# The opening of a Fourier-attention and ELU kernel, laid out anew

## The chip, the cores and the metric

The kernel runs on one core of one Trainium2 chip. The core has five instruction streams that run side by side and meet only at semaphores: TensorE (PE, matrix products into PSUM), VectorE (DVE), ScalarE (ACT), GpSimd (POOL) and SyncE (SP, which here only issues DMAs; POOL and ACT issue some too). The metric is the device time of one launch in microseconds. Before the change three timed runs gave 903.19, 903.33 and 905.1 us, median 903.33.

## What is computed

Two stages. The first mixes each of 8 sequences (3008 positions, 256 channels) in the frequency domain; the second sends the 24064 rows through 256 -> 2048 -> 256 with an ELU between.

```python
X = np.fft.rfft(x, axis=1)
Yr = Xr @ w_r - Xi @ w_i + b_r
Yi = Xr @ w_i + Xi @ w_r + b_i
lam = 0.01                                   # soft threshold of both parts
Yr = np.sign(Yr) * np.maximum(np.abs(Yr) - lam, 0.0)
Yi = np.sign(Yi) * np.maximum(np.abs(Yi) - lam, 0.0)
y = np.fft.irfft(Yr + 1j * Yi, n=x.shape[1], axis=1)
...
h = x @ w_in
g = np.where(h > 0.0, h, np.exp(np.minimum(h, 0.0)) - 1.0)
return (g @ w_out).astype(np.float32)
```

## The kernel before

The transform of length 3008 = 47 x 64 is done as matrix products in two steps each way, with the twiddle factors built into the matrices M1 to M4. For one sequence the work is cut into these units:

- **A** (6 units, `unit_A`, L150): the transform over the 64, two matmuls of 512 columns into two PSUM banks, copied to a tile A. Four j-blocks per unit; two units share one tile A of 8 blocks, and its store to the DRAM tensor DA reorders the data. `load_Z` (L172) reads it back as Z.
- **X** (8 units, `unit_X`, L187): the transform over the 47, eight small matmuls, copied into XT. Two channel halves (dt) times four groups of eight.
- **M** (12 groups, `m_group`, L205 and L210): the product with the weights, 128 rows by 512 columns; then the soft threshold, which gives Y. A tile Y holds two groups. In the opening the threshold is done either as bias in PE, Relu in ACT (L245, `clip`) and a minimum in DVE (L235, done late by `let_go`), or by a DVE add (L220) and two POOL instructions (L248, L249).
- **B** (6 units, L262 or, as `split_B`, L326): the first inverse step, eight matmuls per unit into two banks, copied to a tile Bz (for the first pair of units under the tag A) and stored to DB by SP (L278, L338). `load_Bs` (L295) reads DB back as four tiles Bs.
- **Y** (8 units, L403, L416, L430): the second inverse step, into yT.

The second stage walks 376 steps, 47 for each sequence (a step is one block of 512 rows and one pair of the 16 blocks of 128 hidden columns): `front` (L895) makes the hidden values, ACT takes the exponential (L902 in the first ten steps), POOL or DVE finish the ELU (L948, L937), and `back` (L969), two steps later, adds into the output banks. The work of the next sequence, units A to Y, is dealt out over the steps by `plan`: list `f0` stands before a step's `front`, list `f1` behind it.

The instruction order of each engine is the order in which the source issues it; nothing reorders it. Every engine takes its own list in order, so an instruction that waits holds up all behind it. Tiles come from pools with a tag and a number of buffers: `wk2` has two for each tag (A and Bz among them), `wk3` three, and a tile that reuses a buffer waits for all reads of it, a DMA's landing included. PSUM has eight banks, shared out anew in stages: `pre2` and `pre1` up to the M groups, `lateB`, `chain` and `lateA` after them, then `psO`, `psS0`, `psS1` and `psG`.

The opening is all that comes before the steps of sequence 0 can run: A, X and M of sequence 0, all B units, the first quarter of Y, and the loads and scaling of w_in. The first Y quarter needs rows of all B units; those of B 0, 1 and 2 (48 of the 96 rows, `NT` = 3) are not waited for through DRAM but turned on chip: `turn_B` (L366) makes them with the channels in the partitions, `turn_back` (L385) turns them with the identity into Bs, and only the rows of B 3 to 5 come by `load_Bs(0, 0, 48)`. The order of M groups is 3, 4, 5, 0, 1, 2, with B 3, B 4 and B 5 between them. Then come turn_B(0), group (2, 1), B 0, turn_B(1), B 1 as a split unit, turn_B(2), two turn_backs, a spare A unit of sequence 1 (`spare_A`, L307), first_Y (L403), B 2 (L326), and the steps. In steps 0 to 4 the remaining five A units of sequence 1 run, in steps 7 to 9 the other quarters of Y of sequence 0, and from step 10 on X of sequence 1.

`idle_pe` (L445) are matmuls whose result is not used. `gate` (L750) is a POOL copy of one column, which keeps POOL's next DMA behind the tile that it reads; the second half of w_out (`load_w_out(1)`, L737) is loaded by POOL behind such a gate on Bs.

Of the kernel before, what the change touches and what calls it, by code (L numbers as in the profile page):

```python
# [8 lines left out]
ALU = mybir.AluOpType  # L9
# [20 lines left out]
def kernel(  # L30
# [93 lines left out]
    def evac(dst, src, on_dve):  # L124
        if on_dve:
            nc.vector.tensor_copy(dst, src)
        else:
            nc.scalar.copy(dst, src)  # L128
# [109 lines left out]
    def first_M(q, i, on_act):  # L238

        ps = pre1.tile([P, 2 * D], F32, name="mps1", tag="mps1")  # L240
        yb, clip = m_group(0, q, i, ps[:], on_act)
        let_go()
        Y_ = Y_of[0, q][:, i, :]
        if on_act:
            nc.scalar.activation(clip[:], yb, AF.Relu, bias=lam_n[:])  # L245
            held.append((Y_, yb, clip))
        else:
            nc.gpsimd.tensor_scalar(clip[:], yb, LAM, -LAM, ALU.min, ALU.max)  # L248
            nc.gpsimd.tensor_tensor(Y_, yb, clip[:], ALU.subtract)  # L249

    def unit_B(b, v, alone=False, on_dve=False):
        if (b, v // 2) not in Bz_of:
            t = "A" if alone and v == 0 else "Bz"
            Bz_of[b, v // 2] = wk2.tile([P, 8, D], BF16, name=t, tag=t)
            if b not in DB_of:
                DB_of[b] = dram.tile([K1, P, D], BF16, name="DB", tag="DB")
        Bz, Y = Bz_of[b, v // 2], Y_of.pop((b, v))
        ps = unit_ps("bps", alone)
        for pp in range(2):
            for c in range(2):  # L260
                for s in range(2):
                    nc.tensor.matmul(  # L262
                        ps[:, s, pp * D : pp * D + D],
                        lhsT=M3[s * N2 : s * N2 + N2, 2 * v + pp, c, :],
                        rhs=Y[s * N2 : s * N2 + N2, pp, c * D : c * D + D],
                        start=(c == 0), stop=(c == 1),
                    )
        o = 4 * (v % 2)
        Bv = Bz[:, o : o + 4, :].rearrange("p (q s) d -> p s q d", s=2)
        psv = ps[:].rearrange("p s (q d) -> p s q d", d=D)  # L270
        if on_dve:
            nc.scalar.copy(Bv[:, :, 0], psv[:, :, 0])
            nc.vector.tensor_copy(Bv[:, :, 1], psv[:, :, 1])
        else:
            nc.scalar.copy(Bv, psv)  # L275
        if alone:
            k0 = 4 * v
            nc.sync.dma_start(  # L278
                DB_of[b][k0 : k0 + 4].rearrange("k p d -> p k d"), Bz[:, o : o + 4, :]
            )  # L280
        elif b == 1 and v > 3:
            nc.sync.dma_start(
                DB_of[b][4 * v : 4 * v + 4].rearrange("k p d -> p k d"), Bz[:, o : o + 4, :]
            )
        elif v % 2:
            k0 = 8 * (v // 2)
            nc.sync.dma_start(DB_of[b][k0 : k0 + 8].rearrange("k p d -> p k d"), Bz[:])
# [10 lines left out]
    def two_banks(pool, n):  # L298
        return [pool.tile([P, 512], F32, name=n, tag=n) for _ in range(2)]

    def spare_A():

        A_of[1, 0] = wk2.tile([P, 8, D], BF16, name="A", tag="A")
        DA_of[1] = dram.tile([NJ, P, D], BF16, name="DA", tag="DA")
        ps = two_banks(lateA, "lateA")
        for j in range(2):
            nc.tensor.matmul(  # L307
                ps[j][:], lhsT=M1[:], rhs=xts[0][:, 2 * j : 2 * j + 2, :], start=True, stop=True
            )

        def store():
            for j in range(2):
                evac(
                    A_of[1, 0][:, 2 * j : 2 * j + 2, :].rearrange("p n d -> p (n d)"),
                    ps[j][:], bool(j),
                )

        return store

    def split_B(v, ps, both_dve):  # L320

        Bz, Y = Bz_of[0, v // 2], Y_of.pop((0, v))
        for pp in range(2):
            for c in range(2):
                for s in range(2):
                    nc.tensor.matmul(  # L326
                        ps[s][:, pp * D : pp * D + D],
                        lhsT=M3[s * N2 : s * N2 + N2, 2 * v + pp, c, :],
                        rhs=Y[s * N2 : s * N2 + N2, pp, c * D : c * D + D],
                        start=(c == 0), stop=(c == 1),  # L330
                    )
        o = 4 * (v % 2)
        Bv = Bz[:, o : o + 4, :].rearrange("p (q s) d -> p s q d", s=2)

        def store():
            for s in range(2):
                evac(Bv[:, s], ps[s][:].rearrange("p (q d) -> p q d", d=D), both_dve or bool(s))
            nc.sync.dma_start(  # L338
                DB_of[0][4 * v : 4 * v + 4].rearrange("k p d -> p k d"), Bz[:, o : o + 4, :]
            )  # L340

        return store
# [4 lines left out]
    def one_bank():  # L347
        return chain.tile([P, 512], F32, name="one", tag="one")

    def turn_B(v, ps=None):  # L350

        split = ps is not None

        if not turned:
            turned.append(wk3.tile([P, 2, 8, 16 * NT], BF16, name="yb", tag="yb"))
        Y, T = Y_of[0, v], turned[0]
        if split:
            ps = [t[:, 0:P] for t in ps]
        else:
            both = unit_ps("tps", True)  # L360
            ps = [both[:, s, 0:P] for s in range(2)]
        for pp in range(2):
            for dt in range(2):
                for c in range(2):
                    for s in range(2):
                        nc.tensor.matmul(  # L366
                            ps[s].rearrange("p (t m q g) -> p t q g m", t=2, m=8, q=2)[:, dt, pp],
                            lhsT=Y[
                                s * N2 : s * N2 + N2, pp, c * D + dt * P : c * D + dt * P + P
                            ],  # L370
                            rhs=M3[s * N2 : s * N2 + N2, 2 * v + pp, c, :].rearrange(
                                "p (g m) -> p g m", g=4
                            )[:, :, 0:8],
                            start=(c == 0), stop=(c == 1),
                        )
        Tv = T[:, :, :, 16 * v : 16 * v + 16].rearrange("p t m (q s g) -> p s (t m) q g", q=2, s=2)
        for s in range(2):
            evac(Tv[:, s], ps[s].rearrange("p (n q g) -> p n q g", q=2, g=4), split and bool(s))

    def turn_back(dt):  # L380

# [345 lines left out]
    def load_w_in(q):  # L727
        if q < 3:
            wf = late3.tile([P, 2, FQ], F32, name="w_in_f", tag="Et")
        else:  # L730
            wf = late2.tile([P, 2, FQ], F32, name="w_in_f", tag="osb")
        nc.sync.dma_start(wf[:], w_in_v[:, :, q * FQ : q * FQ + FQ])
        w_in_f.append(wf)
# [19 lines left out]
    def fB(v, on_dve=False):  # L753
        unit_B(0, v, alone=True, on_dve=on_dve)
# [9 lines left out]
    nc.scalar.copy(bias_bc[:], nb[:])  # L764
    idle_pe(5)
    for u in range(8):
        unit_X(0, u, alone=True, on_dve=u in (1, 3, 5), apart=u > 5)
        if u == 3:
            nc.vector.tensor_tensor(w3[:], v3[:], w3[:], ALU.subtract)
        if u < 6:  # L770
            idle_pe(1)
    zeroth.close()
    pre2, pre1 = (
# [30 lines left out]
    fB(4)  # L804
    scale_w_in(0, True, 0)
    first_M(0, 1, True)
    first_M(1, 0, False)
    fB(5)
    load_w_in(2)
    load_Bs(0, 0, 16 * NT)  # L810
    scale_w_in(0, True, 1)
    first_M(1, 1, True)
    first_M(2, 0, True)
    turn_B(0)
    scale_w_in(1, True, 0)
    first_M(2, 1, True)
    fB(0)
    turn_B(1)
    let_go()
    store_B = split_B(1, two_banks(pre1, "mps1"), False)  # L820
    turn_B(2, two_banks(pre1, "mps1"))
    store_B()
    load_w_in(3)
    M4v = M4[:].rearrange("p (a h) -> p a h", h=2)
    for h, w in enumerate((w40, w41)):
# [9 lines left out]
        )  # L835
        for n_, k_ in (("lateB", 2), ("chain", 4), ("lateA", 2))
    )
    turn_back(0)
    turn_back(1)
    keep_A = spare_A()  # L840
    first_Y(0)
    first_Y(1)
    keep_B = split_B(2, two_banks(lateB, "lateB"), False)
    keep_A()
    keep_B()
    scale_w_in(1, True, 1)
    second.close()

# [150 lines left out]
    def plan(b):  # L999
# [40 lines left out]
            if u == ("A", 5) and n2 < B:  # L1040
                f1[t] += [(load_Z, (n2, s0, s1)) for s0, s1 in ((0, 8), (8, NS))]
        if b == 0:
            for t in range(5):
                f1[t].append((unit_A, (1, t + 1, False, t not in (1, 2), True)))
            for t, a, u in (
                (7, f0, 2), (7, f1, 3), (8, f0, 4), (8, f1, 5), (9, f0, 6), (9, f1, 7)
            ):
                a[t].append((split_Y, (0, u)))
            for t, w in ((2, 1), (3, 2), (5, 3)):
                f1[t].append((load_Bs, (0, w)))  # L1050
            f1[5] += [(load_Z, (1, s0, s1)) for s0, s1 in ((0, 8), (8, 16), (16, NS))]
            f1[xs[0]].append((lambda: gate(Z_of[1][:, 16, 0:1]), ()))
        if n2 < B:
# [84 lines left out]
```

## Time and profile before

One execution was profiled: it took 904.25 us, its span from the first to the last instruction is 902.5 us, at a granted TensorE clock of 0.999.

| engine | busy us | share of the span | instructions |
|---|---|---|---|
| PE (matmul) | 884.6 | 98% | 6667 |
| PEld (weight load, beside PE) | 653.5 | 72% | 6770 |
| DVE | 714.4 | 79% | 902 |
| ACT | 696.8 | 77% | 871 |
| POOL | 325.0 | 36% | 464 |

The times of the opening, from the timelines (us from the start of the span):

| what | PE starts at |
|---|---|
| first X unit of sequence 0 | 24.06 |
| first M group | 30.39 |
| turn_back | 47.42 |
| first front of step 0 | 50.29 |
| first X unit of sequence 1 (step 10) | 72.66 |

How to read the lines further down. A row of the timeline is: start, duration (of all together, where several equal instructions are merged), engine, line, operation, tile written <- tiles read, shape, count, and in brackets how long the engine had been idle and what ended that. SPq, POOLq and ACTq rows are the issue of a DMA, not its transfer. A row of the waits is: who waited, for what, us in total, how many times, the longest. A row of a DMA queue is: packets, MB, share of the time of 16 DMA engines.

### The profile page before, as it was taken

How to read it: one execution, taken by the hardware profiler on the slowest of the kernel's cores; microseconds unless marked ns; L12 is line 12 of the kernel's file. 1: busy time of each engine (PE TensorE's matmuls, PEld its weight loads, DVE VectorE, ACT ScalarE, POOL GpSimd, SP SyncE). 2: the span in 40 equal slices, each digit the busy share in tenths (PEclk: the TensorE clock that was granted, in tenths of full speed). 3: DMA queues.
4: the chain of work that ended last, by engine and by line, in shares of the span. 5: the costliest groups of instructions: out<-in, count | busy, mean ns of one | idle time of the engine just before them, and what ended most of it. 6: DMA issues, size and time to landing. Idle time of an engine off the chain costs nothing.

```text
span 902.5 us, 17320 instructions
## 1 busy us (share of the span) xinstructions
PE 884.6 (98%) x6667; PEld 653.5 (72%) x6770; DVE 714.4 (79%) x902; ACT 696.8 (77%) x871; POOL 325.0 (36%) x464
## 2 busy tenths in 40 slices
PE   9899999999999999999999999999999999999997
PEld 4467667876688667876678766787667866777776
DVE  7788768877788778897788877888778877788776
ACT  6788788877878778778887887878787877776664
POOL 7561550134230531404504243133332134443664
PEclk9999999999999999999999999999999999999999
DMA  8996226621473226713266041752128111231011
GB/s 257 325 255 182 86 68 195 190 71 48 124 204 117 71 63 166 206 59 94 60 198 188 25 112 53 213 162 82 55 82 226 31 42 47 75 95 44 24 48 48
DMA packets 90489, 105.80 MB, mean 117 GB/s; under 512 B 5363, under 2 KB 81142, under 8 KB 86982
## 3 DMA queue, kind: packets, MB, share of 16 engines
q1 hardware_dynamic: 84054, 76.64, 30.4%
q0 software_dynamic: 5968, 27.26, 9.2%
q8 instruction: 53, 0.87, 0.4%
q10 hardware_dynamic: 384, 0.79, 0.3%
q14 instruction: 30, 0.25, 0.1%
HBM read 54.86 MB, written 49.81 MB: 116 GB/s over the span
## 4 chain that ended last, share of the span: by engine, by line
PE 88%; DVE 4%; ACT 3%; issue 2%; DMA 1%; POOL 0%; DVEq 0%; ACTq 0%; POOLq 0%
PE ps_o L969 35%; PE hps L895 34%; PE mps L210 9%; PE bps L262 2%; PE aps L150 2%; PE yps L430 2%; PE xps L187 2%; DVE gT L939 1%; DVE Et L950 1%; ACT Et L913 1%; ACT Et L916 1%; ACT Bz L275 1%; PE sps L895 1%; DMA Z<-DA 1%; DMA xt<-in_x_dram 0%
## 5 line engine op out<-in xcount | busy, mean ns | idle before, releaser
L969 PE MATMUL ps_o<-w_out_r,gT 128*128 128x256 f32 x3008 | 475.9, 301 | 0.1
L969 PEld LDWEIGHTS ps_o<-w_out_r,gT 128*128 128x128 f32 x3008 | 403.1, 189 | 49.0 <-DVE osb L981 1.6
L895 PE MATMUL hps<-yT,w_in_s 128*128 128x512 bf16 (+7 forms) x1613 | 372.0, 350 | 5.1 <-DVE gT L939 0.2
L937 DVE SCALAR_TENSOR_TENSOR gT<-Et,hps 128x512 fp32r<-128x512 f32 (+1 forms) x268 | 220.1, 850 | 73.8 <-POOL Et L948 37.5
L939 DVE SCALAR_TENSOR_TENSOR gT<-hps,Et 128x1024 fp32r<-128x1024 f32 x190 | 232.3, 1222 | 16.0 <-DVE Et L950 0.9
L895 PEld LDWEIGHTS <-w_in_s 128*128 128x128 bf16 x1728 | 141.5, 98 | 128.3 <-issue 21.4
L948 POOL TENSOR_SCALAR Et<-Et 128x512 f32<-128x512 f32 x204 | 121.9, 616 | 224.5 <-ACT Et L911 217.0
L916 ACT ACTIVATE Et<-hps 128x1024 f32<-128x1024 f32 x190 | 195.8, 1031 | 8.7 <-PE hps L895 2.3
L950 DVE TENSOR_SCALAR Et<-Et 128x1024 f32<-128x1024 f32 x190 | 131.4, 692 | 44.2 <-ACT Et L916 36.5
L228 POOL TENSOR_SCALAR clip<-yb 128x512 f32<-128x512 f32 x84 | 51.8, 616 | 317.3 <-DVE yb L220 279.8
L911 ACT ACTIVATE Et<-hps 128x512 f32<-128x512 f32 x182 | 98.9, 596 | 62.2 <-PE hps L895 60.5
L913 ACT ACTIVATE Et<-hps 128x1024 f32<-128x1024 f32 x84 | 86.3, 1027 | 71.8 <-PE hps L895 70.3
L229 POOL TENSOR_TENSOR Y<-yb,clip 128x512 bf16<-128x512 f32 x84 | 107.3, 1277 | 7.0
L914 ACT ACTIVATE Et<-Et 128x1024 f32<-128x1024 f32 x84 | 88.8, 1058 | 2.7
L220 DVE TENSOR_TENSOR yb<-mps,bias_bc 128x512 f32<-128x512 f32 x88 | 60.6, 689 | 36.0 <-PE mps L210 24.4
L128 ACT CAST XT<-xps 128x768 bf16<-128x768 f32 x59 | 47.2, 800 | 15.4 <-PE xps L187 15.3
L210 PE MATMUL mps<-wcat_s,XT 128*128 128x512 bf16 x182 | 56.7, 379 | 0.7
L210 PE MATMUL mps<-wcat_r,XT 128*128 128x512 bf16 x179 | 57.0, 384 | 0.4 <-ACT Bz L275 0.4
L128 ACT CAST A<-aps 128x1024 bf16<-128x1024 f32 x42 | 42.5, 1014 | 14.0 <-PE aps L150 12.5
L210 PEld LDWEIGHTS <-XT 128*128 128x128 bf16 x384 | 30.9, 98 | 30.0 <-ACT XT L128 1.2
L128 ACT CAST yT<-yps 128x752 bf16<-128x752 f32 x56 | 44.2, 789 | 9.2 <-PE yps L430 9.1
L275 ACT CAST Bz<-bps 128x1024 bf16<-128x1024 f32 x45 | 45.1, 1002 | 3.6 <-PE bps L262 3.6
(149 smaller groups left out, 463.6 us busy)
## 6 DMA issues: line engine op xcount, KB each, us to landing
xt<-in_x_dram POOLq DMA_DIRECT2D x21, 1024.0 KB, 7.1
out_dram<-osb SPq DMA_DIRECT2D x158, 128.0 KB
Bs<-DB SPq DMA_DIRECT2D x30, 384.0 KB
DA<-A SPq DMA_DIRECT2D x20, 512.0 KB
DB<-Bz SPq DMA_DIRECT2D x20, 512.0 KB
Z<-DA SPq DMA_DIRECT2D x6, 1152.0 KB
xt<-in_x_dram POOLq DMA_DIRECT2D x6, 512.0 KB, 5.7
Z<-DA SPq DMA_DIRECT2D x8, 384.0 KB
```

What stands on the lines that cost most here:

```text
L128: nc.scalar.copy(dst, src)
L210: nc.tensor.matmul(ps, lhsT=XT[:, dt, c, o : o + P], rhs=(wcat_r, wcat_s)[c][:, dt, :], start=(not biased and (c, dt) == (0, 0)), stop=((c ...
L229: nc.gpsimd.tensor_tensor(Y_of[b, q][:, i, :], yb, clip[:], ALU.subtract)
L895: nc.tensor.matmul(hps[s][:, c0:c1] if early else hps[:, s, c0:c1], lhsT=w_in_s[:, dt, ft * P : ft * P + P], rhs=yT_of[b][:, dt, t0 : t0 + ...
L911: nc.scalar.activation(E_[:, s], hps[:, s], AF.Exp)
L913: nc.scalar.activation(E_, hps[:], AF.Relu, scale=-1.0)
L916: nc.scalar.activation(E_, hps[:], AF.Exp)
L937: nc.vector.scalar_tensor_tensor(o, e, -1.0, h, ALU.add, ALU.max)
L939: nc.vector.scalar_tensor_tensor(o, h, 0.0, e, ALU.max, ALU.add)
L948: nc.gpsimd.tensor_scalar(E_[s], E_[s], 1.0, 0.0, ALU.min, ALU.max)
L950: nc.vector.tensor_scalar(E_, E_, 1.0, -1.0, ALU.min, ALU.add)
L969: nc.tensor.matmul(po[q][:, i_ % 2, :], lhsT=gT[:, s, i_ * P : i_ * P + P], rhs=w_out_r[:, ft, :], start=(ft == 0 and i_ % 2 == 0), stop=( ...
```

## The change

X: units 4 to 7 (before: 6 and 7) put their halves into two banks, of which ACT copies one and DVE the other; unit 3 goes from DVE to ACT; the subtraction for w3 comes after unit 1 and not after 3; the fillers after units 4 and 5 are gone.

M and B: B 5 and `load_Bs(0, 0, 48)` come one M group earlier, and the load of w_in's third quarter behind that Bs load in SP's queue. The last group (2, 1) becomes `last_M`: its 512 columns are done as two halves (each holds one channel half of the real and of the imaginary part) in two banks, with a clip and a minimum of its own for each. `load_w_in(3)`, the two M4 rows, the gate and `load_w_out(1)` come right after it, before the pools change. Then, from the late pools: turn_B(1), B 0, turn_B(2) in two channel halves, the store of B 0, B 1, turn_backs, B 2, first_Y, and behind them the stores of B 2 and then of B 1 (both of B 1's copies by DVE). `spare_A` is gone.

Steps: all six A units of sequence 1 lie in steps 0 to 5, and Bs 1, 2 and 3 are loaded in steps 1, 2 and 3 (before: 2, 3 and 5).

```diff
+    def last_M(q, i):
+        XT, o = XT_of[0], (2 * q + i) * P
+        clip = wk2.tile([P, 2 * D], F32, name="clip", tag="clip")
+        todo = []
+        for h, t in enumerate(two_banks(pre1, "mps1")):
+            def cols(v):
+                return v.rearrange("p (c h d) -> p c h d", c=2, h=2)[:, :, h]
+            ps = t[:, 0:D]
+            nc.tensor.matmul(ps, lhsT=busy[:, 0:P], rhs=cols(bias_p[:]), start=True, stop=False)
+            for c in range(2):
+                for dt in range(2):
+                    nc.tensor.matmul(
+                        ps, lhsT=XT[:, dt, c, o : o + P],
+                        rhs=cols((wcat_r, wcat_s)[c][:, dt, :]),
+                        start=False, stop=((c, dt) == (1, 1)),
+                    )
+            ch = clip[:, D * h : D * h + D]
+            nc.scalar.activation(ch, ps, AF.Relu, bias=lam_n[:])
...
+        let_go()
+        for Y_, yb, ch in todo:
+            nc.vector.scalar_tensor_tensor(Y_, yb, LAM, ch, ALU.add, ALU.min)
...
-    def split_B(v, ps, both_dve):
-
+    def split_B(v, ps, on_dve=(False, True)):
+
+        if (0, v // 2) not in Bz_of:
+            t = "A" if v == 0 else "Bz"
+            Bz_of[0, v // 2] = wk2.tile([P, 8, D], BF16, name=t, tag=t)
...
-                evac(Bv[:, s], ps[s][:].rearrange("p (q d) -> p q d", d=D), both_dve or bool(s))
+                evac(Bv[:, s], ps[s][:].rearrange("p (q d) -> p q d", d=D), on_dve[s])
...
-    def turn_B(v, ps=None):
+    def turn_B(v, ts=(0, 1), ps=None, on_dve=False):
...
     for u in range(8):
-        unit_X(0, u, alone=True, on_dve=u in (1, 3, 5), apart=u > 5)
-        if u == 3:
+        unit_X(0, u, alone=True, on_dve=u == 1, apart=u > 3)
+        if u == 1:
             nc.vector.tensor_tensor(w3[:], v3[:], w3[:], ALU.subtract)
-        if u < 6:
+        if u < 4:
             idle_pe(1)
...
     first_M(0, 1, True)
+    fB(5)
+    load_Bs(0, 0, 16 * NT)
+    load_w_in(2)
     first_M(1, 0, False)
-    fB(5)
-    load_w_in(2)
-    load_Bs(0, 0, 16 * NT)
...
     turn_B(0)
     scale_w_in(1, True, 0)
-    first_M(2, 1, True)
-    fB(0)
-    turn_B(1)
-    let_go()
-    store_B = split_B(1, two_banks(pre1, "mps1"), False)
-    turn_B(2, two_banks(pre1, "mps1"))
-    store_B()
+    last_M(2, 1)
     load_w_in(3)
...
+    turn_B(1, ps=two_banks(lateB, "lateB"))
+    store_0 = split_B(0, two_banks(lateA, "lateA"))
+    for t in range(2):
+        turn_B(2, (t,), two_banks(chain, "one"), True)
+    store_0()
+    store_1 = split_B(1, two_banks(lateB, "lateB"), (True, True))
     turn_back(0)
     turn_back(1)
-    keep_A = spare_A()
+    store_2 = split_B(2, two_banks(lateA, "lateA"))
     first_Y(0)
     first_Y(1)
-    keep_B = split_B(2, two_banks(lateB, "lateB"), False)
-    keep_A()
-    keep_B()
+    store_2()
+    store_1()
     scale_w_in(1, True, 1)
...
         if b == 0:
-            for t in range(5):
-                f1[t].append((unit_A, (1, t + 1, False, t not in (1, 2), True)))
+            for t in range(6):
+                f1[t].append((unit_A, (1, t, False, t not in (1, 2), True)))
...
-            for t, w in ((2, 1), (3, 2), (5, 3)):
-                f1[t].append((load_Bs, (0, w)))
+            for w in range(1, 4):
+                f1[w].append((load_Bs, (0, w)))
```

`spare_A` is taken out whole: it made the tile A and the tensor DA of sequence 1, ran the two matmuls of A unit 0 into `lateA` and left the two copies (ACT and DVE) to be done behind first_Y.

More of the change, by code (lines that the diff above doesn't have):

```diff
@@ L249, in first_M @@
             nc.gpsimd.tensor_tensor(Y_, yb, clip[:], ALU.subtract)
+    def last_M(q, i):
[16 more added lines that the diff above has]
+            nc.scalar.activation(ch, ps, AF.Relu, bias=lam_n[:])
+            todo.append(
+                tuple(
+                    v.rearrange("p (c d) -> p c d", c=2) if k else cols(v)
+                    for k, v in enumerate((Y_of[0, q][:, i, :], ps, ch))
+                )
+            )
+        let_go()
+        for Y_, yb, ch in todo:
+            nc.vector.scalar_tensor_tensor(Y_, yb, LAM, ch, ALU.add, ALU.min)
     def unit_B(b, v, alone=False, on_dve=False):
@@ L299, in two_banks @@
         return [pool.tile([P, 512], F32, name=n, tag=n) for _ in range(2)]
[L301 to L318, printed above, removed]
-    def split_B(v, ps, both_dve):
+    def split_B(v, ps, on_dve=(False, True)):
+        if (0, v // 2) not in Bz_of:
+            t = "A" if v == 0 else "Bz"
+            Bz_of[0, v // 2] = wk2.tile([P, 8, D], BF16, name=t, tag=t)
+            if 0 not in DB_of:
+                DB_of[0] = dram.tile([K1, P, D], BF16, name="DB", tag="DB")
         Bz, Y = Bz_of[0, v // 2], Y_of.pop((0, v))
@@ L348, in one_bank @@
         return chain.tile([P, 512], F32, name="one", tag="one")
-    def turn_B(v, ps=None):
-        split = ps is not None
+    def turn_B(v, ts=(0, 1), ps=None, on_dve=False):
         if not turned:
@@ L356, in turn_B @@
         Y, T = Y_of[0, v], turned[0]
+        w = len(ts) * 64
+        split = ps is not None
         if split:
-            ps = [t[:, 0:P] for t in ps]
+            ps = [t[:, 0:w] for t in ps]
         else:
             both = unit_ps("tps", True)
-            ps = [both[:, s, 0:P] for s in range(2)]
+            ps = [both[:, s, 0:w] for s in range(2)]
         for pp in range(2):
-            for dt in range(2):
+            for dt in ts:
                 for c in range(2):
@@ L366, in turn_B @@
                         nc.tensor.matmul(
-                            ps[s].rearrange("p (t m q g) -> p t q g m", t=2, m=8, q=2)[:, dt, pp],
+                            ps[s].rearrange("p (t m q g) -> p t q g m", m=8, q=2, g=4)[
+                                :, dt - ts[0], pp
+                            ],
                             lhsT=Y[
@@ L375, in turn_B @@
                         )
-        Tv = T[:, :, :, 16 * v : 16 * v + 16].rearrange("p t m (q s g) -> p s (t m) q g", q=2, s=2)
+        Tv = T[:, ts[0] : ts[-1] + 1, :, 16 * v : 16 * v + 16].rearrange(
+            "p t m (q s g) -> p s (t m) q g", q=2, s=2
+        )
         for s in range(2):
-            evac(Tv[:, s], ps[s].rearrange("p (n q g) -> p n q g", q=2, g=4), split and bool(s))
+            evac(Tv[:, s], ps[s].rearrange("p (n q g) -> p n q g", q=2, g=4), on_dve and bool(s))
     def turn_back(dt):
```

## The prediction

> **What bounds the kernel now.** First the page's part 1 and the windows: PE is busy 884.6 of 902.5 us at a granted clock of 1.00, so from the eleventh step on (72.66 us) every engine is paced by PE, and an edit of the opening can only shift that body as a whole. So the sum asks one thing: at what time does the first X unit of the next batch start, 72.66 us now? Then PE's waits between 20 and 75 us, which are all the opening has to give:
>
> ```profile
> PE mps L205 <- DVE XT L126: 1.1, 1, 1.1
> PE xps L187 <- DMA Z<-DA: 0.8, 2, 0.4
> PE one L385 <- DVE yb L126: 0.5, 1, 0.5
> PE mps L366 <- DVE Y L235: 0.3, 1, 0.3
> PE gps L150 <- ACT A L128: 0.2, 1, 0.2
> PE xps L187 <- DVE yT L126: 0.2, 1, 0.2
> ```
>
> (us in total, times, longest.) The longest is the first M group waiting for DVE's copies of X. DVE's timeline there (start, us) shows w3's subtraction and the last whole copy behind it, then two half copies that end at 30.33; PE goes on at 30.39:
>
> ```profile
> 27.59 0.95 DVE L769 TENSOR_TENSOR A<-Bz,A 128x768 f32<-128x768 f32 x1
> 28.46 0.95 DVE L126 CAST XT<-xps 128x768 bf16<-128x768 f32 x1
> 29.32 1.01 DVE L126 CAST XT<-mps 128x384 bf16<-128x384 f32 x2
> ```
>
> Next the DMA queues, since B's stores move. SP's timeline, with POOL's one row for the second half of w_out (1 MB) and ACT's copies of step 2:
>
> ```profile
> 46.68 0.36 SPq L278 DMA_DIRECT2D DB<-A  x1
> 47.94 0.36 SPq L338 DMA_DIRECT2D DB<-A  x1
> 48.34 0.50 SPq L732 DMA_DIRECT2D w_in_f<-in_moe_w_in_dram  x1
> 51.62 0.36 SPq L338 DMA_DIRECT2D DB<-Bz  x1
> 52.84 4.81 SPq L165 DMA_DIRECT2D DA<-A  x2
> 57.82 0.46 SPq L295 DMA_DIRECT2D Bs<-DB  x1
> ```
>
> ```profile
> 48.28 0.98 POOL L737 DMA_DIRECT2D w_out_r<-in_moe_w_out_dram  x1 [0.28 <-issue]
> ```
>
> ```profile
> 55.22 1.09 ACT L902 ACTIVATE Et<-sps 128x512 f32<-128x512 f32 x2 [0.44 <-PE sps L895]
> 56.19 1.08 ACT L128 CAST A<-gps 128x512 bf16<-128x512 f32 x2
> ```
>
> B 0 and 1 leave at 46.68 and 47.94, ahead of w_out; B 2 leaves at 51.62, behind it. What that means is in the DMA view of 52.6 to 54.7 us, where B 2's 512 packets had been issued and w_out's were moving:
>
> ```profile
> q0 software_dynamic: 648, 0.66, 128.5%
> q1 hardware_dynamic: 3, 0.00, 0.3%
> ```
>
> POOL's queue (q0) moved 648 packets and SP's (q1) three. And the whole stretch from 44.0 to 56.4, in which DMA had hardly a pause:
>
> ```profile
> DMA packets 3473, 3.21 MB, mean 259 GB/s; under 512 B 123, under 2 KB 2912, under 8 KB 3472
> ```
>
> **The change part by part.** *X by two engines.* (Before, DVE copies u 1, 3 and 5 whole and half of 6 and 7.) u 3 goes to ACT whole (0.80), u 4 to 7 become halves; the two 0.22 us fillers behind u 4 and 5 filled a wait and cost nothing gone. PE still meets u 4 at 27.33 (the Z wait stays). DVE then has L769 done by 27.1 and four halves, 0.46 us apart by the row of 1.01 for two, the first at 27.9: 27.9 + 3 x 0.46 + 0.55 = 29.83 in place of 30.33. ACT's halves (0.86 for two) end sooner. Gain 0.5. Bounds: 0 if u 6 and 7, which reuse the banks of u 4 and 5, wait longer for them, 1.1 if the whole wait went; 0.5, since I can count it.
>
> *M groups, B 5 one group earlier.* Same PE rows. B 5 stands at about 39.25; its Y is ready at 39.43 - 0.5 = 38.9: no wait. The load of Bs (0,0) then leaves ahead of w_in 2 in SP's queue, about 0.7 us sooner (it waits for B 5's store, which is behind B 4's), and is no longer behind w_in 2's transfer, worth as much again. First_Y has 1.5 us of room. Cost 0; without that cover 0.7 at most.
>
> *Last M group in halves, B 0 to 2 in its waits.* Ten matmuls of 256 for five of 512 is the same 1.08 us. ACT's clip (0.69) and DVE's min (0.69) become two halves of about 0.48 and 0.42 (estimates: the slope of the rows of 512 and 1024), so the first half of turn_B(2) starts 0.3 us sooner; the 0.76 us that PE idles from 45 to 48 (busy 2.24 of 3.00) is met by B 0 and B 1, which stood before it, so it is mostly moved. In order, by rows: last M ends 44.35 (44.87 - 0.5); turn 0.23, B 0 0.54 with a wait of 0.5 for a bank and Y, turn 2 0.23 with 0.3, B 1 0.43, turn_back 0.95, B 2 0.54, first_Y 0.7, and 0.4 of wait for yT: step 0 starts at 49.3, not 50.29. Gain 1.0 up to here, of which 0.57 is the spare A unit that left. Bounds: 0.4 to 1.5 (the waits of 0.5 and 0.3 kept or gone).
>
> *A units in steps 0 to 5.* One more unit lies in the steps: 52.87 to 53.45, 0.58 of PE. B 1's store is now two DVE copies (0.68 each, 0.60 apart) ahead of the first gT, where before one of them went to ACT sooner: back(0) waits 0.45. Cost 1.0; bounds 0.6 and 1.7 (all 1.2 us of DVE exposed). So far -1.0 + 1.0 = 0.0.
>
> *The new wait.* A of batch 1 takes its tile from tag A, two buffers; the third unit (index 2) writes the buffer that B 0 and B 1 were stored from, so ACT's copy waits until both stores have landed. Before, both had left by 48.3 and those copies ran from 53.61, unhindered. Now B 1's store leaves last of all, behind B 2's: B 1's two copies end at 51.4. At step 2 ACT would be free for the copy at 55.7 (Exp 55.22 + 1.09 = 56.3 before, 0.6 sooner now). When does B 1 land? Bs, w_in 2 and 3, w_out, B 0, B 2 and B 1 are 0.20 + 2 x 0.52 + 1.05 + 3 x 0.26 = 3.08 MB, the first packet about 0.9 us after Bs is issued at 44.1. At 259 GB/s that is 11.9 us: 45.0 + 11.9 = 56.9, and about 0.8 for the landing (B 5: issued 42.32, and the load waiting for it left at 44.75, of which only a part is transfer): 57.7. ACT stands in order: the third unit's copies, then the next Exp, so the fourth A unit gets no bank on PE, and back(1) is queued behind that on PE; DVE's and POOL's work for step 3 follows. Cost 57.7 - 55.7 = 2.0, one for one. Bounds: 0 (B 1 issued 51.46, plus the 2.4 us that B 5's store took: 53.9, no wait) and 3.5 (B 2 took up to 57.82 - 51.62 = 6.2 us; one store more behind it, 51.46 + 6.2 + 1.2 = 58.9, and 0.3). I take the first-come reading, because the view of 52.6 to 54.7 shows SP's packets standing still while w_out moves.
>
> [...]
>
> Sum: 902.5 + 0.0 + 2.0 = 904.5 us of span; the profiled run took 904.25, so 906.3 on that footing. The three timed runs have 903.33 as median, 0.9 below the profiled one, and I forecast for the median: 903.33 + 2.0 = **905.3**.
>
> **The rivals.**
> 1. *The wait is covered.* B 1 lands by 55.7, since queues share or w_out leaves early enough. For it: w_out is issued about 1.4 us sooner, as Bs is. Against: the 3 packets, and that the bytes are the same. Then 903.33 + 0.0 = 903.3, no change.
> 2. *A faster kernel.* Place: the tail of the opening and steps 0 to 5. If the three waits that I left in the tail (0.5, 0.3, 0.4) vanished and the extra A unit lay in what PE idles from 50.29 to 72.66 (22.37 - 21.88 = 0.49), with B 1 landed in time: -1.0 - 1.2 + (0.58 - 0.49) = -2.1: 901.2. It decides only if no wait is handed on; against it, each A unit now stands behind a wait for its bank or close to one (the 0.2 at L150).
> 3. *A second wait behind the first.* The load of Bs (0,1) waits in SP's order for the same landing, then A's last store (step 5 in place of 4) and Z. Before, that store left at 60.91, Z at 66.04, first needed at 72.66. Now the store leaves at about 65.1; plus 5.1 for Z's issue and about 3.9 for its first quarter gives 74.1 against 74.7. If each takes 1 us longer, X waits 1.4: 906.7.
>
> **How the numbers follow.** Forecast 0.55 (own range 904.2 to 906.8, by landings from 56.6 to 59.2), rival 1 0.20, rival 2 0.06, rival 3 0.19. About 0.2%, 1.8 us, is what a measurement of this kernel can tell from no change, so 905.13 divides: of the forecast's 0.55 some 0.38 lie above it and 0.17 below. Slower 0.38 + 0.19 = 0.57, same 0.17 + 0.20 = 0.37, faster 0.06. The range holds rivals 1 and 3 with the unknown costs: 902.8 to 907.4.
>
> **What would show it.** The first M group's bias matmul at about 29.9; step 0's first matmul at about 49.3; ACT idle before the third A unit's copy at step 2, released by a DMA of DB, for about 2 us, and PE idle as long before the fourth A unit; X of the next batch at about 74.7. Wrong if that copy has no DMA in front of it (rival 1), if step 0 starts later than 49.8, or if PE waits for Z at step 10 (rival 3).

## The result and the profile after

The changed kernel takes 906.82 us (median of 15 runs, 904.15 to 908.73), the kernel before 904.28 on the same chips (15 runs, 903.19 to 905.10): a ratio of 1.0029, 95% interval 1.0020 to 1.0038, so 1.8 to 3.4 us slower. The profiled execution has a span of 906.7 us and took 908.44, near the upper end of its runs; the profile before had 902.5 and 904.25, at the middle of its own. So the 4.2 us between the two profiles are more than the 2.5 us between the medians, and that has to be explained too. One run of x_alone, an experiment below, took 992.48 us at a mean granted clock of 0.851, the only one of all runs above 909 us, and its ratio leaves that run out.

PE's waits from 20 to 75 us, after (us in total, times, longest):

```profile
PE gps L150 <- ACT A L128: 2.7, 1, 2.7
PE xps L187 <- DMA Z<-DA: 0.8, 1, 0.8
PE mps L205 <- DVE XT L126: 0.7, 1, 0.7
PE mps L187 <- ACT XT L128: 0.5, 1, 0.5
PE lateA L342 <- DVE Y L235: 0.3, 1, 0.3
```

The wait at the M group fell from 1.1 to 0.7, the 0.5 at turn_back is gone, one of 0.5 for ACT's copies in the X units has come, and a new one stands first: PE waits 2.7 us for ACT to free the banks of an A unit (PE's L150). The timeline of DVE in the X units shows w3's subtraction (L789) early and then only half copies, the last in time for the bias matmul at 29.70:

```profile
25.52 0.95 DVE L789 TENSOR_TENSOR A<-Bz,A 128x768 f32<-128x768 f32 x1
27.27 1.02 DVE L126 CAST XT<-mps 128x384 bf16<-128x384 f32 x2 [0.80 <-PE mps L187]
28.62 1.02 DVE L126 CAST XT<-mps 128x384 bf16<-128x384 f32 x2 [0.33 <-PE mps L187]
```

Timelines of SP, POOL (one row) and ACT (one row), after:

```profile
47.15 0.37 SPq L354 DMA_DIRECT2D DB<-A  x1
50.18 0.37 SPq L354 DMA_DIRECT2D DB<-Bz  x1
51.33 0.36 SPq L354 DMA_DIRECT2D DB<-A  x1
53.81 0.36 SPq L165 DMA_DIRECT2D DA<-A  x1
58.52 0.79 SPq L325 DMA_DIRECT2D Bs<-DB  x2
```

```profile
47.48 0.98 POOL L757 DMA_DIRECT2D w_out_r<-in_moe_w_out_dram  x1 [0.28 <-issue]
```

```profile
58.54 1.07 ACT L128 CAST A<-gps 128x512 bf16<-128x512 f32 x2 [2.75 <-DMA DB<-A]
```

Here is the cause by name. The third A unit's copy is ready at 55.8 and starts at 58.54, when a store of DB from tile A has landed: B 1's, issued at 51.33, 7.2 us before. The load of Bs, which waits for the same landing, leaves SP at 58.52. The DMA view says what lay in front of that store. First the queue rows of 51 to 53 us (B 2's store had been issued at 50.18), then of 52.6 to 54.7, the stretch shown of before (POOL's queue is q0, SP's q1; packets, MB, share of 16 engines):

```profile
q0 software_dynamic: 513, 0.53, 120.1%
```

```profile
q0 software_dynamic: 411, 0.41, 78.0%
q1 hardware_dynamic: 520, 0.26, 41.7%
```

For two microseconds w_out moves alone, and then both queues move side by side. Last, PE after the wait, in its timeline and in the table by stretches (the stretch and its length; busy us and counts of PE, PEld, DVE, ACT and POOL; PE's granted clock; DMA's share and GB/s):

```profile
59.18 1.17 PE L150 MATMUL gps<-xt,M 128*128 128x512 f32 x2 [2.75 <-ACT A L128]
60.15 1.91 PE L988 MATMUL ps_o<-w_out_r,gT 128*128 128x256 f32 x8
61.87 1.72 PE L914 MATMUL sps<-yT,w_in_s 128*128 128x512 bf16 x4
```

```profile
56.00:59.00 3.00, 0.44 (x3) 0.00 (x0) 1.29 (x2) 0.46 (x1) 1.44 (x3) 1.00 0.46 135
59.00:60.00 1.00, 0.82 (x2) 0.52 (x3) 0.00 (x0) 1.00 (x4) 0.00 (x0) 0.91 0.69 109
60.00:61.00 1.00, 1.00 (x5) 0.91 (x5) 0.61 (x1) 1.00 (x3) 0.80 (x2) 0.50 0.77 242
63.00:64.00 1.00, 1.00 (x6) 0.72 (x5) 0.00 (x0) 0.96 (x2) 0.34 (x1) 0.88 1.15 317
```

(Between 61 and 63 the clock is 0.50 as well.) Four matmuls of L914 take 1.72 us there and 1.04 elsewhere. By the shares of 0.91 and 0.88 the low stretch runs from 59.82 to 63.24, 3.42 us, and at half the clock a PE that is always busy loses, by estimate, half of it: 1.71 us.

So the opening, by three marks that all executions have:

| us | before | after |
|---|---|---|
| first X unit to first M group's bias matmul | 6.33 (24.06 to 30.39) | 6.16 (23.54 to 29.70) |
| bias matmul to step 0's first matmul | 19.90 | 19.50 |
| step 0 to X of the next sequence | 22.37 (to 72.66) | 27.77 (to 76.97) |

All of the loss is in the steps: 5.4 us, of which 2.75 are the wait and 1.71 the clock.

### The profile page after: what moved, and what is told of

The parts are those of the page before. It is cut to its first block, busy times and chain, and to the rows that moved or that the text cites. A ratio compares the mean times of both kernels' runs of the same rounds, so it can differ in the third digit from the quotient of the medians.

```text
span 906.7 us, 17334 instructions
## 1 busy us (share of the span) xinstructions
PE 885.6 (98%) x6670; PEld 654.0 (72%) x6773; DVE 714.7 (79%) x906; ACT 697.2 (77%) x874; POOL 327.1 (36%) x464
## 4 chain that ended last, share of the span: by engine, by line
PE 85%; DVE 4%; ACT 4%; issue 3%; DMA 3%; POOL 1%; DVEq 0%; SPq 0%; ACTq 0%; POOLq 0%
PE ps_o L988 35%; PE hps L914 33%; PE mps L210 8%; PE bps L292 2%; PE yps L450 2%; PE aps L150 2%; PE xps L187 2%; DVE gT L958 1%; DVE Et L969 1%; ACT Et L935 1%; ACT Et L932 1%; DMA DB<-A 1%; DMA xt<-in_x_dram 1%; DMA Z<-DA 1%; ACT Bz L305 1%
## 5 line engine op out<-in xcount | busy, mean ns | idle before, releaser
L988 PEld LDWEIGHTS ps_o<-w_out_r,gT 128*128 128x128 f32 x3008 | 403.8, 189 | 49.3 <-DVE osb L1000 1.6
L914 PE MATMUL hps<-yT,w_in_s 128*128 128x512 bf16 (+7 forms) x1613 | 371.9, 350 | 5.1
L914 PEld LDWEIGHTS <-w_in_s 128*128 128x128 bf16 x1728 | 141.7, 98 | 129.1 <-issue 21.9
L210 PE MATMUL mps<-wcat_r,XT 128*128 128x512 bf16 x176 | 55.8, 384 | 0.3 <-ACT Bz L305 0.3
```

The lines of the kernel that those rows point to most:

```text
L210: nc.tensor.matmul(ps, lhsT=XT[:, dt, c, o : o + P], rhs=(wcat_r, wcat_s)[c][:, dt, :], start=(not biased and (c, dt) == (0, 0)), stop=((c ...
L914: nc.tensor.matmul(hps[s][:, c0:c1] if early else hps[:, s, c0:c1], lhsT=w_in_s[:, dt, ft * P : ft * P + P], rhs=yT_of[b][:, dt, t0 : t0 + ...
L988: nc.tensor.matmul(po[q][:, i_ % 2, :], lhsT=gT[:, s, i_ * P : i_ * P + P], rhs=w_out_r[:, ft, :], start=(ft == 0 and i_ % 2 == 0), stop=( ...
```

## The experiments

Each one is an edit of the changed kernel unless it says otherwise; "steps" is the time from step 0's first matmul to the next sequence's first X unit (before 22.37, after 27.77), which is free of what the start of an execution adds. The ratios are to the kernel before, run beside each of them, with medians from 903.75 to 904.48 us.

**own_tile: the wait taken away by another buffer.**

```diff
-                A_of[b, ci] = wk2.tile([P, 8, D], BF16, name="A", tag="A")
+                pool = own if (b, ci) == (1, 1) else wk2
+                A_of[b, ci] = pool.tile([P, 8, D], BF16, name="A", tag="A")
...
+    own = ctx.enter_context(tc.tile_pool(name="own", bufs=1))
```

> The changed kernel with one edit: A units 2 and 3 of batch 1 write a tile of their own, so ACT's copy at step 2 no longer waits for B 0 and B 1 to be stored. Theory (the wait on B 1's landing is the whole loss, 2.75 us in the changed kernel's trace, and what PE then ran at a clock of 0.50 from 60 to 63 us, some 1.6 us, is its consequence): no DMA in front of the third A unit's copy, PE's clock 1.00 throughout 55 to 66 us, X of the next batch at about 72.7 (76.97 less 4.3), the time back at the kernel's before, 904.3 within 0.7, and the spread of its runs as narrow as there (2 us, not 4.6). Rival (the loss is the sixth A unit in the steps and the two DVE copies, whatever the wait does): X at 75 or later and 905.8 or more.

Measured: 903.95 us (903.68 to 905.15), ratio 0.9996 (0.9988 to 1.0005). ACT's copy has no DMA in front of it, the clock is 1.00 in every stretch, steps 23.27. B 1 lands as late as ever (SP's next load leaves at 58.99), and nobody on PE's path waits for it. So the wait and what follows from it are the whole loss; the sixth A unit and the two DVE copies cost 23.27 - 22.37 = 0.90. X itself stood at 73.14, 0.4 later than expected, because in that execution PE had waited 1.50 us for Z before the opening's third X unit.

**w_out_late: the bytes taken out of the store's way.** POOL issues w_out's second half in step 1.

```diff
     gate(Bs_of[0, 0][64:96, 0, 0:1])
-    load_w_out(1)
...
+            f1[1].append((load_w_out, (1,)))
```

> The changed kernel with the load of w_out's second half (1 MB) issued by POOL in step 1, not ahead of the opening's tail, so that B 2's and B 1's stores are in their queue some 2 us ahead of its first packet. w_out is first needed at back(4), after 65 us. Theory (B 1 lands late because w_out's bytes, which were issued first, go first): B 2 and B 1 land as B 0 did, 2.5 to 3.7 us after their issue, B 1 by 55.2; no wait at the third A unit, X at about 72.7 and 904.3 within 0.8. Rival 1 (each store takes as long whatever lies ahead, because queues share): B 1 still lands after 57 us, the wait is 1.5 to 2.75 and the time 906 to 907. Rival 2 (w_out is then late itself): PE waits at back(4) for w_out and the time is 906 or more.

Measured: 903.68 us (903.19 to 904.64), ratio 0.9994 (0.9986 to 1.0003); no wait, steps 23.42. SP's timeline gives the landing:

```profile
50.95 0.36 SPq L354 DMA_DIRECT2D DB<-A  x1
...
53.88 1.53 SPq L325 DMA_DIRECT2D Bs<-DB  x2
```

The Bs load, which waits for B 1, follows 2.9 us after its store and not 7.2. The store itself, its copies and its place behind B 2 are the changed kernel's. w_out was not late for back(4). The same run shows the order a second time, on a store that nobody waits for: sequence 1's first store of A is issued by SP at 53.42, behind w_out (51.68), and from 53.5 to 57.0 us the queue rows are POOL's alone:

```profile
q0 software_dynamic: 729, 0.75, 97.8%
```

**b1_first: the two stores in the other order.** `store_1()` ahead of `store_2()`.

> The changed kernel with the two stores in the other order: B 1's copies and store ahead of B 2's. B 1 is issued at about 50.8 in place of 51.33 and has 512 packets less of SP's queue ahead of it; B 2, on which no copy waits, leaves last. Theory (what counts is the landing of the store that the third A unit's buffer was read by, behind w_out): B 1 lands about 1.5 us sooner, 56.8 to 57.3, the wait is 1.0 to 1.6 us, too short for the clock to fall, and the time 905.3 to 906.0. Rival (the two stores share the engines and land together): the wait stays at 2.4 us or more, and the time at 906.5 or more.

Measured: 905.51 us (904.18 to 908.81), ratio 1.0014 (1.0004 to 1.0023). ACT waits 0.63 us for DB and copies at 56.39, the clock stays at 1.00, steps 24.39. The theory's direction holds and the landing is somewhat earlier than it said; another 0.7 us went to a wait for B 2's DVE copy, which now stands later.

**w_out_half: half of the bytes.** 0.5 of the 1 MB ahead of the tail, the rest in step 1.

```diff
+        if part < 2:
+            hf = slice((2 + part) * NFT // 4, (3 + part) * NFT // 4)
...
-    load_w_out(1)
+    load_w_out(1, 0)
...
+            f1[1].append((load_w_out, (1, 1)))
```

> The changed kernel with only half of w_out's second half (0.5 of 1 MB) loaded ahead of the opening's tail, and the rest issued in step 1. Theory (B 1's landing is late by the bytes of w_out that are ahead of it): 0.5 MB less at 260 to 340 GB/s is 1.5 to 1.9 us, so B 1 lands at 56.1 to 57.0 on the clock of the first profile (step 0 at 49.20), the wait at the third A unit is 0.3 to 1.3 us and the clock does not fall, as with the wait of 0.63 in the variant with B 1 first; X 23.7 to 24.7 us after step 0's start, 904.3 to 905.4. Rival (what delays the store is that POOL's queue is active at all, not its bytes): the wait stays at 2 us or more, and 906 or more.

Measured: 903.31 us (902.98 to 907.42), ratio 0.9990 (0.9981 to 0.9999); no wait, steps 23.42. B 1 landed 3.35 us after its issue at the latest (54.99 to 58.34), 3.8 sooner after its issue than with the whole megabyte, and not 1.5 to 1.9. SP's rows:

```profile
54.99 0.36 SPq L354 DMA_DIRECT2D DB<-A  x1
...
58.34 1.76 SPq L325 DMA_DIRECT2D Bs<-DB  x2
```

The rival falls, but the size of the theory does too: taking half of the bytes away took nearly all of the delay away. One part of a reason is how much of the load was still to come when B 1 was issued. Here 0.43 MB of it had moved between w_out's issue and B 1's (51.24 to 54.99):

```profile
q0 software_dynamic: 423, 0.43, 46.4%
```

That leaves 0.1 MB; in after 220 of its packets, 0.23 of 1 MB, had moved by then (51.33), which leaves 0.8. The difference of 0.7 MB, at the 263 GB/s of 51 to 53 us in after, is 2.7 of the 3.8 us by estimate. Bytes left are no full account, though: in the second profile of the changed kernel only 14 packets had moved when B 1 was issued, and it landed 6.4 us later, not 7.2 or more. And in after, from 56 to 59 us, with w_out done, the DMA engines were busy for 0.46 of the time only, and B 1 landed at 58.5 all the same. No run shows why.

Its profile fell in the longest of its runs, and shows by accident what follows a wait elsewhere. PE waits 1.88 us for Z in the X units, and then (timeline row and stretches):

```profile
26.97 0.51 PE L187 MATMUL xps<-M,Z 96*128 96x96 bf16 x8 [1.88 <-DMA Z<-DA]
```

```profile
28.00:30.00 2.00, 1.82 (x27) 1.58 (x24) 1.11 (x2) 1.82 (x5) 1.92 (x4) 0.61 0.53 114
30.00:32.00 2.00, 1.35 (x14) 0.94 (x12) 1.25 (x3) 1.84 (x4) 0.64 (x1) 0.50 0.99 369
34.00:36.00 2.00, 2.00 (x8) 0.78 (x7) 1.21 (x2) 0.83 (x2) 0.00 (x0) 0.68 1.07 426
```

The clock is low from 28.44 to 35.28, 6.84 us, and bias matmul to step 0 takes 21.32 and not 19.50.

**again: the changed kernel profiled once more.**

> The changed kernel as it is, one more profile. Open is whether the fall of PE's clock belongs to the wait or to chance. If it comes whenever PE idles for some 2.7 us, this profile has a stretch at 0.50 after the wait, and X stands 27.5 to 28 us after step 0's start (27.77 in the first profile). If it depends on where the idle stretch falls, it may be absent, with the wait unchanged: then X stands about 26.1 us after step 0's start.

Measured: 907.64 us, span 905.8. The wait is 2.00 us, the clock falls again (0.98 from 56 to 59, 0.50 to 61, 0.68 to 63: low from 58.88 to 62.28, 3.40 us), steps 26.87. So in two profiles of two. ACT's row:

```profile
58.04 1.07 ACT L128 CAST A<-gps 128x512 bf16<-128x512 f32 x2 [2.00 <-DMA DB<-A]
```

**filler and filler_4: PE kept busy in the wait.** Eight, or four, matmuls on a bank that nothing reads, ahead of the fourth A unit.

```diff
+    def fill(k):
+        bank = two_banks(psS0, "sps")[0]
+        for _ in range(k):
+            nc.tensor.matmul(bank[:], lhsT=busy[:, 0:P], rhs=busy[:], start=True, stop=True)
...
+            f1[3].insert(0, (fill, (8,)))
```

> The changed kernel with eight filler matmuls of 512 columns (8 x 0.22 = 1.76 us) on PE ahead of the fourth A unit, in the stretch in which PE stood idle for 2.75 us; they wait for the first Exp's bank to be read, about 57.3 us. The wait on the DMA stays. Theory (the half clock from 60 to 63 us follows from PE's idling and costs about 1.6 us in the executions in which it comes): clock 1.00 in every stretch of 55 to 66 us, eight matmuls of L988 in 1.1 us and not 1.91; ACT still waits about 2.75 us for DB; the slowest runs fall from 908.7 to about 907.2, the median by 0.5 to 1.0. Rival (the slow PE is no matter of idling, but of the DMA traffic or of waits between the matmuls): the clock row still shows 0.50 and the time is the changed kernel's or more, as fillers that outlast the wait add up to 1 us.

> The changed kernel with four filler matmuls (0.88 us) in the wait in place of eight. With eight the clock stayed at 1.00 beside a wait of 2.76 us, but their lowest time was 905.58 where the changed kernel's is 904.15: where B 1 lands early they outlast the wait. Theory (the clock's fall is most of what lies above the wait): with four the clock stays at 1.00 in the profile, the fillers end about 58.2, ahead of most landings, and the median is 905.3 to 906.2, below both 906.6 (eight) and 906.8 (none). Rival (the clock falls all the same, since PE still idles some 1.9 us in two pieces): a stretch at 0.50 behind the wait, and 906.5 or more.

Measured: 906.59 us (905.58 to 907.99), ratio 1.0027 (1.0016 to 1.0038), with eight; 906.96 (904.83 to 908.69), 1.0029 (1.0018 to 1.0041), with four. With eight:

```profile
58.01 1.07 ACT L128 CAST A<-gps 128x512 bf16<-128x512 f32 x2 [2.76 <-DMA DB<-A]
```

The wait is the changed kernel's to 0.01 us, the clock is 1.00 from 53 to 66, steps 26.18. With four the wait is 2.07 (its row names a PE instruction as releaser; SP's load, which waits for the same landing, leaves 0.02 us before the copy starts), the clock 1.00, steps 25.45. Own_tile's 23.27 plus the wait, plus 1.71 where the clock fell, meets all four profiles:

| profile | wait | clock | sum | steps measured |
|---|---|---|---|---|
| after | 2.75 | fell | 27.73 | 27.77 |
| again | 2.00 | fell | 26.97 | 26.87 |
| filler | 2.76 | 1.00 | 26.03 | 26.18 |
| filler_4 | 2.07 | 1.00 | 25.34 | 25.45 |

So in a profile the fall costs what the clock row says, and was absent where PE had work (from 56 to 59 us PE was busy for 2.24 us with eight fillers and 2.00 with four, where it is 0.44 in after and 1.00 in again). The medians did not follow: both expectations of a lower median missed. In what share of the executions the clock falls is open. A fall of 3.4 us takes 0.002 off the mean clock over 906 us, so it was absent in the seven of the changed kernel's 15 runs whose mean clock reads 1.000 (median 906.34); the seven at 0.998 or 0.996 have 907.74, but the kernel before reads 0.998 at times too, so not all of these need have had one. Both profiles of the changed kernel (908.44 and 907.64) lie above its median, which is why their openings lose more than the medians do.

**x_alone and steps_alone: one part of the change put into the kernel before.** The first has only the X units' edit, the second no spare A unit, A units 0 to 5 in steps 0 to 5 and Bs in steps 1 to 3.

> The kernel before with the change's X part alone (X's last four units copied by both engines, the fillers behind u 4 and 5 left out, w3's subtraction behind u 1). Theory (from the third X unit to the first M group's bias matmul the changed kernel and its four variants all took 4.10 us, the kernel before 4.93, of which 0.43 was a wait for Z): 4.10 here too, so the bias matmul stands 0.5 to 0.8 us sooner; the gain is handed through to step 0 and the time is 903.5 to 904.1 beside a before of 904.5. Rival (the waits behind take the gain back, as B's stores, which gate the first load of Bs, do not move with it): step 0 no sooner after Z's landing and 904.5.

> The kernel before with the schedule part alone: no spare A unit in the opening, A units 0 to 5 in steps 0 to 5, the loads of Bs in steps 1 to 3. The third unit's copy writes the buffer of B 0 and B 1 at step 2 here too, but both stores leave by 48.3, ahead of w_out, and landed by 50.4 in the trace of before. Theory (the wait needs both parts: the tile's early reuse and B 1's store behind w_out): no DMA in front of the third A unit's copy, step 0 starts 0.5 us sooner, the steps up to X take 0.7 to 1.0 more than 22.37 us, and the time is 904.5 to 905.1. Rival (the schedule alone brings the loss): a wait of over 1 us at the third A unit and 906 or more.

Measured: x_alone 903.91 us, ratio 1.0002 (0.9993 to 1.0011). From the third X unit to the bias matmul it took 4.62 us, not 4.10: the fourth unit waited 0.18 for DVE and the fifth 0.41 for Z. The bias matmul stands 0.48 sooner than in the profile before, but 0.40 of that is an earlier first X unit (23.66 against 24.06). What stands there is handed on whole (19.91 and 22.38 behind it, X at 72.20 against 72.66), but the times do not tell it from nothing. Steps_alone 903.98 us, ratio 1.0001 (0.9992 to 1.0010): step 0 0.12 us sooner after the bias matmul, steps 22.60, no DMA in front of the third A unit's copy at 55.57. The early reuse of the tile is harmless where B 1's store leaves before w_out (47.69 there, w_out after it). The wait needs both parts.

**best and scale_on_pool: towards a faster version.** Both are w_out_late, with the last scaling of w_in (0.42 us on DVE) taken from ahead of the first gT: behind it in the first, to POOL in the second.

```diff
+    scale_w_in(1, False, 1)
...
-    scale_w_in(1, True, 1)
     second.close()
```

(scale_on_pool; in the other the new line stands in step 1 and is on DVE.)

> The changed kernel with w_out's second half issued in step 1, as in the variant that did so, and the last scaling of w_in (0.42 us on DVE) put behind the first gT in place of ahead of it; it is first needed by step 2's matmuls. Theory (back(0) waits for DVE, which has B 1's two copies, that scaling and the A unit's copy ahead of the first gT): back(0) starts about 0.4 us sooner after step 0's start (3.69 us there), the steps up to X take 23.0 and not 23.42 us, and the time is 903.1 to 903.5, below both kernels. Rival (gT waits for POOL's min of Et or the Exp, not for DVE): no change against 903.7.

> The changed kernel with w_out's second half issued in step 1, as before, and the last scaling of w_in moved from DVE to POOL, where it takes about 1.7 us of the 3.1 that POOL idles ahead of the first Et. (Put behind the first gT it made step 1's Exp wait 1.63 us: Et's second tile is the buffer of the w_in piece that it reads.) Theory: back(0) starts 3.36 us after step 0, as in that variant, the Exp of step 1 waits for nothing but its matmuls, the steps up to X take about 23.05 us, and the time is 903.2 to 903.8. Rival (POOL's reads slow the copies of yT beside it): step 0 starts more than 19.6 us after the first M group's bias matmul, and the gain is gone.

Measured: best 904.38 us, ratio 1.0006 (0.9997 to 1.0014), a miss. back(0) did start 3.36 us after step 0, but the steps took 23.74 and not 23.0, and ACT shows where that was given back:

```profile
52.31 1.08 ACT L919 ACTIVATE Et<-sps 128x512 f32<-128x512 f32 x2 [1.63 <-DVE gT L954]
```

Step 1's Exp writes Et's second tile, which is the buffer of the w_in quarter that the moved scaling reads (three buffers, three quarters before the first Et). The row names gT, which ends at 52.22; the scaling stands right behind it on DVE, at 52.14, takes 0.42 us and had not ended when the Exp began. So the wait came with the moved scaling (w_out_late has none at this Exp), and the shared buffer is the likely reason, which would be the pattern of the change again; but that the Exp waited for the scaling itself is not shown. With the scaling on POOL, scale_on_pool takes 903.22 us (902.16 to 904.26), ratio 0.9990 (0.9982 to 0.9999): steps 23.07, back(0) at 3.35, step 0 19.62 behind the bias matmul, 0.12 more than in the others. It and w_out_half are below the kernel before by about 0.9 us by their ratios, by the intervals 0.1 to 1.7, and by 0.5 in the medians; between the two nothing is decided.

## Why the prediction was right, and where its sum was off

Slower was forecast with 0.57, and it is slower, by the mechanism named. 2.0 us were forecast against the kernel before and 2.5 measured; of the 1.5 between 905.3 and 906.82, 0.95 is the footing (903.33 as median of three runs, 904.28 of fifteen) and 0.5 is the change. That 2.0 and 2.5 lie so close is in part luck. By the ratios, the wait with what follows it costs about 3.0 us (1.0029 against own_tile's 0.9996), 1.0 above the forecast, and the rest of the change gains about 0.4, which own_tile's interval does not tell from the 0.0 of the forecast.

- *X by two engines, gain 0.5*: right within what the profiles tell. From third X unit to bias matmul 4.10 us in every variant with the whole edit and a full clock; before 4.93 with 0.43 of waiting for Z inside, 4.78 in steps_alone without, so 0.7. It shows only when Z is in time (PE waited 0.78 for Z in the profile after, 1.50 in own_tile), and x_alone's times do not resolve it.
- *M groups and B 5 earlier, cost 0*: PE waits for no Bs in the profile after, so the cost is 0 there. But the load of Bs did not leave sooner by the 0.7 that this part was to give: B 5's store was issued 1.5 us sooner (40.79 against 42.32), the load behind it 0.5 (44.24 against 44.75), and counted from the bias matmul not sooner at all (14.54 against 14.36); in the second profile it left at 45.37. The part was not run by itself.
- *Last M group in halves*: step 0 at 49.20, forecast 49.3; behind the bias matmul the gain is 0.40 where 0.5 was forecast. The prediction put 0.57 of its gain down to the spare A unit; steps_alone, which takes that unit out and leaves the last M group whole, gains 0.12 there.
- *A units in steps 0 to 5, cost 1.0*: 0.90 (own_tile) to 1.05 (w_out_late). The shares were others: steps_alone puts the sixth unit and the earlier loads of Bs at 0.23, where 0.58 was forecast for the unit.
- *The new wait, 2.0*: the place, the tile, the releaser and the consumer on PE were all as forecast; in four profiles the wait was 2.75, 2.00, 2.76 and 2.07. The landing, 57.7 by the sum of bytes, came at 58.5 and, in the second profile, 58.0. But the model behind the number was too simple: w_out_half shows that the delay does not go by the size of the load ahead (B 1 landed 7.2 us after its issue behind 1 MB, 3.35 behind half of it, 2.9 with none of it ahead).
- *First-come against sharing*: from 51 to 53 us, behind B 2's issue, the rows show w_out alone, 513 packets against none, and in w_out_late 729 against none; there the load that was issued first went first, as the prediction read it from 648 packets against 3. From 52.6 to 54.7, 520 packets of SP's queue moved beside 411 of w_out's. In what order each engine took them is not shown; the rows do not tell the engines apart. Rival 1 took no wait from sharing; the wait was 2.75 us.
- *What was missing*: that PE's idling would cost more than its own length. The prediction priced the wait "one for one"; in both profiles of the changed kernel the clock then fell to 0.50 for 3.4 us, 1.7 more. This is the term by which X came at 76.97 and not at 74.7.
- *Rival 1* (the wait is covered) fell as it stood; own_tile and w_out_late are what it would have given, 903.95 and 903.68. *Rival 3* fell too: at step 10 PE waits 0.17 us, for DVE's copy of yT, and not for Z. *Rival 2* would have needed waits of the tail to vanish, and 0.33 and 0.23 of them are there (DVE's Y, ACT's yT).

## What to carry to other kernels

When a store is moved later, ask who writes its source tile next: with two buffers in rotation the next writer can be two units on, on another engine, and waits for the landing, not the issue (here at 58.54, for a store issued at 51.33). Then look at what large load has been issued ahead of the store in any queue; here moving one load of 1 MB past the store, or splitting it, was worth as much as another buffer (ratios 0.9994 and 0.9990, and 0.9996). An engine that is the bound should be priced for more than the idle stretch itself if its clock can fall behind it (here a wait of 2.75 us, and 1.71 more by estimate).

## What the hardware showed

PE's granted clock fell to 0.50 after idle stretches of 1.88 (w_out_half), 2.00 (again) and 2.75 us (after), and stayed for 6.84, 3.40 and 3.42 us; after one of 1.50 (own_tile, waiting for Z) it did not fall. The single stretch is not all that differs: in the 3.41 us (the mean length of the two short falls) ahead of the three falls PE was busy for 1.53, 1.41 and 0.66 us in all, and in own_tile for 1.91 from 24.28 to 27.69, around its wait. Four cases set no threshold. The two short falls differ by 0.02 us, and the long one is twice as long; why, no run shows.
